# The first stage of a fused forward and backward kernel, put in another order

## The chip, the cores and the metric

The kernel runs on one core of a Trainium2 chip. A time is the device time of one execution in microseconds (us); the time of a kernel is the median over its runs. The core has five engines that take their instructions in a fixed order each: TensorE (PE, matrix products; PEld is its weight load), VectorE (DVE), ScalarE (ACT), GpSimd (POOL) and SyncE (SP), which here only issues DMA transfers. Instructions on different engines meet through semaphores.

## What is computed

The reference is a block with two branches, its output and the gradients with respect to every input. Cut to what matters:

```python
mod = (silu(c) @ w_mod).reshape(1, 6, 1, -1)
sa, ca, ga, sb, cb, gb = (mod[:, k] for k in range(6))
h = layernorm(x) * (1 + ca) + sa
x = x + ga * A(h)          # A: rfft2, times w_r + i w_i, irfft2
h = layernorm(x) * (1 + cb) + sb
x = x + gb * B(h)          # B: layernorm, w1 + b1, gelu, w2 + b2
out, vjp = jax.vjp(block, x, w_r, w_i, w1, b1, w2, b2, c, w_mod)
return out, *vjp(grad_out)
```

x and grad_out are 2048 x 1024, w_r and w_i 2048 x 513, w1 1024 x 3584, w2 3584 x 1024, w_mod 1024 x 6144, all bf16.

## The kernel before, in words

Everything is written for one core and runs as one stream of 6835 matmuls on PE with the other engines around it. A scheduler orders each engine's instructions by the program's text, by priorities (`tc.high_priority()` puts an instruction ahead) and by explicit edges: `tc.issue_after(ins)` puts what follows behind `ins` on its own engine. `nc.any` lets the scheduler choose between DVE and ACT. Tiles with the same tag share a buffer: a later one waits for the readers of the earlier one.

**The conditioning rows.** `mod_block(r, h)` (L247) multiplies the vector silu(c), spread over 128 partitions (`u_b`), with one 1 MB block of w_mod (`wblk`, a ring of three slots) into `pm`: eight matmuls (L253) and a copy (L256) to a row. r = 0 is sa, 1 is 1 + ca (`opca_row`), 2 ga, 3 sb, 4 1 + cb, 5 gb. All twelve blocks are loaded on SP's queue.

**The scaled copies of grad_out.** grad_out comes in four tiles `go` of 1 MB. PE turns each with 32 transposes of 128x128 into `pt` (L344). Each evicted tile is multiplied on the way by gb as a column (`gb_col`, from eight tiny matmuls `pc`, L337): even chunks by DVE (L347), odd ones by ACT (L351), 16 each. The result is `gBoT`, grad_out times gb, transposed.

**pp, the filler.** `ph_part(fc, js)` multiplies w2, transposed while it is loaded (`load_w2t`, L301, a DMA transpose on SP's queue into `wt`, two slots), with gBoT: eight matmuls (L684) for each of 28 chunks fc and four blocks j, 896 in all. An eviction (L691, L694) writes the tile to `pho`, and POOL's queue stores it to `d_ph` (L696). The first six chunks are the text ahead of the spectral stage, most of the others keep PE busy beside it.

**The row blocks of x.** `load_tok(i)` loads 512 rows of x: 256 directly by SP (L128), 256 gathered in reversed order by two indirect DMAs on POOL's queue (L131). For each block: mean and variance (`ln_dve` on DVE alone, L447; `ln_mix` half by DVE and half by ACT as sums and squares, L451 and L454), a square root on ACT (L427), the normalization on ACT (`norm_act`, L461, four per block), the product with 1 + ca on DVE, eight folds of 128x2048 on DVE (`fold_tok`, `fold_d`, all recorded at L173), and the addition of the folded sa (`saf`). The result is `fbuf[:, i]`.

**The matrices.** Sines and cosines of the transform are generated: POOL multiplies indices (L373), DVE takes them modulo a power of two (L396), ACT takes the sine (L397); eight 128x1024 passes into `smA`, `smB`, four 128x512 passes into `em1`, which POOL then scales (L412). They are stored to `d_SF` and `d_E`.

**The spectral stage** (`spectral_core`) begins with the products `pu` (L472) of the matrices with all four `fbuf` blocks, so it can begin only when the last block is folded. Then come pairs, `pv` and `po`; `consume_fwd(i)` takes each of four output blocks through two layer norms (on DVE and ACT, `ct` and `xt` tiles) and stores `d_x1` and `d_n3`.

**The MLP stage** follows a plan by hand, and PE's matmuls are strictly ordered there: z(0,0), the last 64 pp matmuls (fc 24 to 27, j = 2 and 3), z(0,1), z(0,2), z(0,3), b(0,0), z(0,4), b(0,1), z(0,5) and on. `z_block(b, g)` is 4 x 8 matmuls `pz` (L802) in two plus two PSUM banks; ACT evicts each with its bias (L805), squares (L807) and takes two sigmoids (L811, L813); DVE does the products of the gelu and its derivative, among them hh = sg * zb. Its five work tiles (`gt`) alternate between two sets. b(b, k) are parts of the product of hh with w2 (`pbo`, L853).

ACT holds one set of function tables at a time: sine, square root and sigmoid each need a table load (ACT_TABLE_LOAD) when another set is in.

Of the kernel before, what the change touches and what calls it, by code (L numbers as in the profile page):

```python
# [17 lines left out]
P = 128  # L18
# [17 lines left out]
def kernel(  # L36
# [88 lines left out]

    def load_tok(t4, src, i, eng=None):
        s3 = tok_flat(src)
        ins = (eng or nc.sync).dma_start(out=t4[:, 0:4:3, :],  # L128
                          in_=bass.AP(tensor=s3.tensor, offset=s3.offset + 128 * i * D, ap=[[D, P], [1024 * D, 2], [1, D]]))
        for q in range(2):  # L130
            nc.gpsimd.indirect_dma_start(out=t4[:, 1 + q, :], out_offset=None, in_=s3,  # L131
                                         in_offset=bass.IndirectOffsetOnAxis(ap=xidx[:, 2 * i + q:2 * i + q + 1], axis=0))
        return ins
# [113 lines left out]
    def mod_block(r, h, wblk=None):  # L247
# [4 lines left out]
        for jc in range(NDC):  # L252
            nc.tensor.matmul(pm[:], lhsT=u_b[:, jc, :], rhs=wblk[:, jc, :], start=(jc == 0), stop=(jc == NDC - 1))  # L253
        dst = MOD_DST[r][:, h * KH:(h + 1) * KH]
        with tc.high_priority():
            nc.any.tensor_copy(out=dst, in_=pm[:])  # L256
        if r in (1, 4):
            nc.vector.tensor_scalar(out=dst, in0=dst, scalar1=1.0, scalar2=None, op0=ALU.add)

# [40 lines left out]
    def load_w2t(fg):  # L300
# [4 lines left out]
    gos = [reg.tile([P, 4, D], BF16, name="go0", tag="px1")[:], reg.tile([P, 4, D], BF16, name="go1", tag="smb")[:],  # L305
           fbuf[:, 2], fbuf[:, 3]]
# [10 lines left out]
    mod_get(1, 0)  # L317
    load_tok(x4s[0], A_x, 0)
    mod_get(1, 1)
    mod_get(5, 0)  # L320
    for h in range(2):
        mod_block(1, h, wm[1, h][:])
    mod_get(5, 1)
    load_go(0)
    load_w2t(0)
    load_go(1)
    load_tok(x4s[1], A_x, 1)
    load_go(2)
    load_go(3)
    for h in range(2):  # L330
        mod_block(5, h, wm[5, h][:])
    load_tok(x4s[2], A_x, 2)
    load_tok(x4s[3], A_x, 3)
    load_w2t(1)
    pc = ps_d("pc")
    for cch in range(NDC):
        nc.tensor.matmul(pc[:, cch:cch + 1], lhsT=gb_row[0:1, cch * P:(cch + 1) * P], rhs=ones_bf[0:1, 0:1], start=True, stop=True)  # L337
    with tc.high_priority():
        nc.vector.tensor_copy(out=gb_col[:], in_=pc[:, 0:NDC])
    for j in range(4):  # L340
        for cch in range(NDC):
            pt = psum.tile([P, BW], BF16, tag="f", name="pt", bufs=4)
            for a in range(4):
                nc.tensor.transpose(pt[:, a * P:(a + 1) * P], gos[j][:, a, cch * P:(cch + 1) * P], ident[:])  # L344
            if cch % 2 == 0:
                with tc.high_priority():
                    nc.vector.tensor_scalar(out=gBoT[j][:, cch, :], in0=pt[:], scalar1=gb_col[:, cch:cch + 1], scalar2=0.0,  # L347
                                            op0=ALU.mult, op1=ALU.add, accum_out=gu[:, j, cch:cch + 1])
            else:
                with tc.high_priority():  # L350
                    nc.scalar.activation(out=gBoT[j][:, cch, :], in_=pt[:], func=ACT.Identity, scale=gb_col[:, cch:cch + 1],  # L351
                                         accum_out=gu[:, j, cch:cch + 1])

# [17 lines left out]
    def pts(out, in0, s1, s2, o0, o1=None):  # L371
        kw = {} if o1 is None else {"op1": o1}
        nc.gpsimd.tensor_scalar(out=out, in0=in0, scalar1=s1, scalar2=s2, op0=o0, **kw)  # L373
# [15 lines left out]
    def trig(dst, colv, rowv, nrow, width, modn, cosine):  # L389
# [3 lines left out]
        for r in range(nrow):  # L393
            pts(idx[:, r * width:(r + 1) * width], colv, rowv[:, r:r + 1], sh, ALU.mult, ALU.add)
        n = nrow * width
        nc.vector.tensor_scalar(out=idx[:, 0:n], in0=idx[:, 0:n], scalar1=modn - 1, scalar2=None, op0=ALU.bitwise_and)  # L396
        nc.scalar.activation(out=dst, in_=idx[:, 0:n].rearrange("p (r w) -> p r w", w=width), func=ACT.Sin,  # L397
                             bias=negpi[:], scale=2 * np.pi / modn)
# [5 lines left out]
    def gen_mats():  # L404
        for cl, colv, modn in ((CE, kevc, 2048), (SE, kev, 2048), (CO, kod, 4096), (SO, kod, 4096)):
            sm = (smA, smB)[cl % 2]
            for i2 in range(2):
                trig(sm[:, cl // 2, 2 * i2:2 * i2 + 2, :], colv, rown[:, 2 * i2:2 * i2 + 2], 2, 512, modn, cl < 2)
            nc.gpsimd.dma_start(out=d_SF[:, cl], in_=sm[:, cl // 2])
        for cl, colv, modn in ((CE, jf[:, 0:256], 1024), (SE, jf[:, 1:257], 1024), (CO, jod, 2048), (SO, jod, 2048)):  # L410
            trig(em1[:, 0, 2 * cl:2 * cl + 2, :], colv, rowd, 2, 256, modn, cl < 2)
        nc.gpsimd.tensor_scalar(out=em1[:, 1], in0=em1[:, 0], scalar1=2.0 / (S * D), scalar2=None, op0=ALU.mult)  # L412
        nc.gpsimd.tensor_scalar(out=em1[:, 1, 0:2, 0:1], in0=em1[:, 0, 0:2, 0:1], scalar1=1.0 / (S * D), scalar2=None, op0=ALU.mult)
        nc.gpsimd.tensor_scalar(out=em1[:, 1, 4:6, 255:256], in0=em1[:, 0, 4:6, 255:256], scalar1=1.0 / (S * D), scalar2=None, op0=ALU.mult)
        nc.gpsimd.dma_start(out=d_E[:], in_=em1[:])
# [42 lines left out]
    def norm_act(out4, in4, row, i):  # L458
        for q in range(4):
            t = 4 * i + q  # L460
            nc.scalar.activation(out=out4[:, q, :], in_=in4[:, q, :], func=ACT.Identity,  # L461
                                 scale=stats[:, row, 0, t:t + 1], bias=stats[:, row, 1, t:t + 1])
# [193 lines left out]
    for h in range(2):  # L656
        mod_block(0, h)
    gen_mats()
# [5 lines left out]
    nc.gpsimd.dma_start(out=out_7.rearrange("(c p) -> c p", p=P), in_=gb2r)  # L664
# [702 lines left out]
```

## Time and profile before

| | us |
|---|---|
| median of 3 runs (1461.4, 1461.49, 1465.73) | 1461.49 |
| the profiled execution | 1459.13 |
| its span in the trace | 1457.3 |
| its mean granted PE clock | 0.992 |

The profiled execution is 1.8 us longer than the span that the trace covers, and 2.4 us shorter than the median. Times inside the kernel are us from the start of the span.

The first stage, in the order of events:

| event | from | to |
|---|---|---|
| first pm matmuls, after 3.97 us of waiting for wblk | 6.32 | 9.89 |
| eight gathers of x issued on POOL | 4.74 | 14.57 |
| SP issues w2T for chunks 0 and 1 | 11.19 | 24.07 |
| transposes of grad_out on PE | 21.6 | 44.9 |
| first pp matmuls | 45.36 | |
| em scaled on POOL | 62.24 | 67.84 |
| norms of block 3 of x on ACT | 111.00 | 115.64 |
| last add into fbuf on DVE | 127.58 | 128.27 |
| first pu matmuls | 129.41 | |
| z(0,0) on PE | 343.87 | 350.77 |
| z(0,4) on PE | 389.19 | 396.10 |

A timeline row reads: start, duration, engine, line, operation, output<-input, shapes, how many instructions are put together in it, and in brackets how long the engine was idle before it and what released it.

### The profile page before, as it was taken

The numbers are of one execution on the slowest core, as the hardware profiler recorded it, in microseconds if no ns is written. First come the engines' busy times: TensorE is split into PE (matmuls) and PEld (weight loads), VectorE is DVE, ScalarE is ACT, GpSimd is POOL, SyncE is SP. The second block draws the span as 40 slices with busy tenths as digits, with TensorE's granted clock in tenths as the row PEclk, the third lists the DMA queues.
The fourth block names the chain that finished last, engine by engine and source line by source line (L and its number), as shares of the span: only waits on it lengthen the run. The fifth ranks groups of instructions, "written<-read, shape, count | busy, mean of one in ns | idle before, by whom it ended". The sixth has DMA issues, their size and how long they took to land. (4 is left out here: it accounts for less than half of the span.)

```text
span 1457.3 us, 18411 instructions
## 1 busy us (share of the span) xinstructions
PE 1396.5 (96%) x6835; PEld 649.0 (45%) x6835; DVE 1058.4 (73%) x1483; ACT 752.2 (52%) x1065; POOL 366.1 (25%) x441
## 2 busy tenths in 40 slices
PE   5889999999999999999999999999999999999997
PEld 2434545444444444444444444344444445444443
DVE  5884786898799787887520889898467678898650
ACT  4675555857887766665305574342622434344211
POOL 6520451211112122122211011021245441222432
PEclk8999999999999999999999999999999999999999
DMA  9962473899887877697998275297699987766991
GB/s 333 286 214 70 142 235 115 270 255 337 257 203 278 259 250 233 201 264 241 277 297 245 74 271 185 107 270 176 181 217 254 254 233 213 194 191 180 297 279 65
DMA packets 358367, 324.28 MB, mean 223 GB/s; under 512 B 209386, under 2 KB 301056, under 8 KB 358022
## 3 DMA queue, kind: packets, MB, share of 16 engines
q1 hardware_dynamic: 324166, 207.71, 52.7%
q0 software_dynamic: 34112, 115.41, 22.6%
q8 instruction: 53, 0.87, 0.2%
q14 instruction: 36, 0.29, 0.1%
HBM read 162.06 MB, written 111.20 MB: 188 GB/s over the span
## 5 line engine op out<-in xcount | busy, mean ns | idle before, releaser
L684 PE MATMUL pp<-gBoT,wt 128*128 128x512 bf16 x896 | 197.9, 380 | 4.5 <-DMA wt<-in_B_w_dram 2.6
L950 PE MATMUL pg<-w1T,gzr 128*128 128x512 bf16 x896 | 197.1, 381 | 0.2 <-ACT gn3b L961 0.2
L1266 PE MATMUL gw1acc<-gzh,n3n 128*128 128x512 bf16 x896 | 195.4, 379 | 1.3 <-DMA gzh<-d_gz 1.3
L684 PEld LDWEIGHTS <-wt 128*128 128x128 bf16 x896 | 87.7, 98 | 109.4 <-issue 4.2
L950 PEld LDWEIGHTS <-gzr 128*128 128x128 bf16 x896 | 87.3, 98 | 108.7 <-issue 6.6
L802 PEld LDWEIGHTS <-w 128*128 128x128 bf16 x896 | 87.3, 98 | 108.8 <-issue 4.7
L1266 PEld LDWEIGHTS <-n3n 128*128 128x128 bf16 x896 | 87.4, 98 | 106.1 <-issue 2.7
L802 PE MATMUL pz<-n3Tb,w 128*128 128x512 bf16 x448 | 99.2, 379 | 1.6 <-DVE w2sD L875 1.4
L802 PE MATMUL pz<-n3Ta,w 128*128 128x512 bf16 x448 | 98.7, 379 | 1.1 <-ACT gt L805 1.1
L1075 PE MATMUL gw2acc<-gB,hhsA 128*128 128x512 bf16 x448 | 98.5, 379 | 1.0 <-DMA hhsA<-d_hh 1.0
L853 PEld LDWEIGHTS <-hhA 128*128 128x128 bf16 x608 | 59.0, 98 | 71.7 <-issue 1.4
L805 ACT ACTIVATE gt<-pz,b_col 128x512 bf16<-128x512 f32 x112 | 72.5, 684 | 34.2 <-PE pz L802 32.8
L1270 ACT CAST gwo<-gw1acc 128x512 bf16<-128x512 f32 x50 | 29.1, 583 | 113.6 <-PE gw1acc L1266 99.0
L173 DVE TENSOR_TENSOR gt<-gt,gt 128x2048 bf16<-128x2048 bf16 x56 | 68.3, 1223 | 22.4 <-ACT gt L813 21.2
L1082 ACT CAST gwo<-gw2acc 128x512 bf16<-128x512 f32 x46 | 26.7, 583 | 109.9 <-PE gw2acc L1075 75.6
L811 ACT ACTIVATE gt<-gt 128x2048 bf16<-128x2048 bf16 x28 | 53.5, 1910 | 55.7 <-DVE gt L173 55.7
L173 DVE TENSOR_TENSOR ct<-ct 128x2048 bf16<-128x2048 bf16 x64 | 75.9, 1218 | 1.8 <-DMA d_n<-ct 1.1
L1075 PEld LDWEIGHTS <-hhsA 128*128 128x128 bf16 x448 | 43.6, 98 | 53.0 <-DMA hhsA<-d_hh 1.7
L997 DVE CUSTOM_DVE_ANT_0 otl<-otl 128x1024 bf16<-128x1024 bf16 x24 | 29.1, 1223 | 49.9 <-DMA otl<-in_w_mod_dram 44.2
L807 ACT ACTIVATE gt<-gt 128x2048 bf16<-128x2048 bf16 x28 | 53.4, 1908 | 5.4 <-DVE hhC L173 2.5
L813 ACT ACTIVATE gt<-gt 128x2048 bf16<-128x2048 bf16 x28 | 53.5, 1909 | 0.5
L1271 POOL DMA_DIRECT2D out_dram<-gwo x56 | 30.6, 548 | 85.6 <-ACT gwo L1270 53.4
(325 smaller groups left out, 2531.5 us busy)
## 6 DMA issues: line engine op xcount, KB each, us to landing
gzr<-d_gz SPq DMA_DIRECT2D x28, 512.0 KB
wblk<-in_w_mod_dram SPq DMA_DIRECT2D x12, 1024.0 KB
out_dram<-otl POOLq DMA_DIRECT2D x48, 256.0 KB
out_dram<-gwo POOLq DMA_DIRECT2D x96, 128.0 KB
d_ph<-pho POOLq DMA_DIRECT2D x21, 512.0 KB
d_hh<-hhA POOLq DMA_DIRECT2D x19, 512.0 KB
w2sD<-in_B_w_dram SPq DMA_DIRECT2D x14, 512.0 KB
hhC<-d_ph SPq DMA_DIRECT2D x14, 512.0 KB
```

Of the source, the lines that this page charges most:

```text
L173: return nc.vector.tensor_tensor(out=out, in0=a, in1=b, op=op)
L684: last_pe[0] = nc.tensor.matmul(pp[:], lhsT=wt[:, fg % 2, cch, k * P:(k + 1) * P], rhs=gBoT[j][:, cch, :], start=(cch == 0), stop=(cch == ...
L802: last_pe[0] = nc.tensor.matmul(pz[:], lhsT=w1s[g][:, cch, k * P:(k + 1) * P], rhs=n3T[:, cch, :], start=(cch == 0), stop=(cch == NDC - 1))
L805: nc.scalar.activation(out=zb[:, k, :], in_=pz[:], func=ACT.Identity, bias=b1_col[:, fc:fc + 1], scale=1.0)
L807: nc.scalar.activation(out=av, in_=zb, func=ACT.Square)
L811: nc.scalar.activation(out=sg, in_=bv, func=ACT.Sigmoid, scale=2.0 * GK)
L813: nc.scalar.activation(out=bv, in_=bv, func=ACT.Sigmoid, scale=-2.0 * GK)
L853: last_pe[0] = nc.tensor.matmul(pbs[i][:], lhsT=hh[:, k, i * P:(i + 1) * P], rhs=wp[:, k, :], start=False, stop=(g == 6 and k == 3))
L950: last_pg[0] = nc.tensor.matmul(pgs[i][:], lhsT=gzs[b, g][:, k, i * P:(i + 1) * P], rhs=w1Ts[g][:, k, h * KH:(h + 1) * KH], start=(g == 0 ...
L1075: nc.tensor.matmul(acc[:], lhsT=hh_of(fc)[:, t, :], rhs=gBs[t // 4][:, t % 4, h * KH:(h + 1) * KH], start=(t == 0), stop=(t == NT - 1))
L1266: nc.tensor.matmul(acc[:], lhsT=n3ns[t // 4][:, t % 4, cch * P:(cch + 1) * P], rhs=gz2[t // 8][:, t % 8, :], start=(t == 0), stop=(t == NT ...
L1271: nc.gpsimd.dma_start(out=out_4[cch * P:(cch + 1) * P, fg * 512:(fg + 1) * 512], in_=ob)
```

## The change

- SP's order: both blocks of gb's row first, then x's block 0, the four tiles of grad_out, the two blocks of 1 + ca, w2T 0, x's blocks 1 to 3, w2T 1, and then the blocks of sa.
- POOL makes the index passes of four of the sine matrices first, and then issues the eight gathers of x.
- ACT takes four sines, then makes its 16 scaled copies, and only then block 0's norm. The copies of gb's second block and of 1 + ca are DVE's.
- pp for chunks 0 and 1 alternate (j by j), right behind the two blocks of 1 + ca on PE. All pp evictions of the first eight chunks are ACT's; `nc.any` remains for the others.
- The blocks of sa follow chunk 1; the six late conditioning blocks come in twos after chunks 3, 4 and 5, where they came in threes after chunks 3 and 5. ACT copies these.
- The matrices are generated in parts: four passes at the start, four after block 1's norm, the four of em1 after block 2's. The four stores to d_SF stand behind them in the text. ACT scales em1, where POOL did.
- Block 1 of x has its statistics from DVE alone. Explicit edges put block i's statistics and norm behind block i - 1's folds and norm.
- saf is added to the blocks 0 and 1 together after block 1.
- The zeroing of `css` goes from POOL to DVE, behind the last fold; the store of out_7 goes behind that of d_E; the slots of the grad_out tiles change.

```diff
-    mod_get(1, 0)
-    load_tok(x4s[0], A_x, 0)
-    mod_get(1, 1)
     mod_get(5, 0)
-    for h in range(2):
-        mod_block(1, h, wm[1, h][:])
     mod_get(5, 1)
-    load_go(0)
-    load_w2t(0)
-    load_go(1)
-    load_tok(x4s[1], A_x, 1)
-    load_go(2)
-    load_go(3)
...
+    rows_of = gen_rows()
+    for _ in range(4):
+        next(rows_of)
+    with tc.issue_after(gen_in["pool"].ins):
+        load_tok(x4s[0], A_x, 0)
+    for j in range(4):
+        load_go(j)
+    for h in range(2):
+        mod_get(1, h)
+    load_w2t(0)
+    mod_block(5, 0, wm[5, 0][:])
+    with tc.issue_after(gen_in["dve"].ins):
+        mod_block(5, 1, wm[5, 1][:], nc.vector.tensor_copy)
...
+            if j % 2 == 0:
+                with tc.high_priority():
+                    (nc.scalar.copy if fc < 8 else nc.any.tensor_copy)(out=ov, in_=pv)
...
+            else:
+                with tc.high_priority(), tc.issue_after(act_in.ins):
+                    act = nc.scalar.activation(out=gBoT[j][:, cch, :], in_=pt[:], func=ACT.Identity, scale=gb_col[:, cch:cch + 1],
+                                               accum_out=gu[:, j, cch:cch + 1])
...
+    for j in range(4):
+        act_in, go_dve = go_turned(j)
+    with tc.issue_after(act_in.ins), tc.issue_after(gbc_in.ins):
+        ln_dve(x4s[0], 0, 0)
+        act_go = norm_act(fbuf[:, 0], x4s[0], 0, 0)
+    with tc.issue_after(gen_in["pool"].ins):
+        for i in range(1, 4):
+            load_tok(x4s[i], A_x, i)
+    x_gathers = g_in[0]
+    with ordered():
+        for h in range(2):
+            last_pe[0] = mod_block(1, h, wm[1, h][:], nc.vector.tensor_copy)
+    for j in range(4):
+        for fc in range(2):
+            ph_part(fc, (j,))
+    load_w2t(1)
...
     for fc in range(PH_EARLY):
-        ph_part(fc, (0, 1, 2, 3))
+        if fc > 1:
+            ph_part(fc, (0, 1, 2, 3))
+        if fc == 1:
+            with ordered():
+                for h in range(2):
+                    last_pe[0] = mod_block(0, h, wm[0, h][:], nc.scalar.copy)
...
         if fc % 2 == 1:
             load_w2t(fc // 2 + 2)
-            if fc > 1:
-                with tc.issue_after(last_pe[0].ins):
-                    for r, h in late_mods[3 * (fc // 2 - 1):3 * (fc // 2)]:
-                        mod_block(r, h)
-
+        if fc > 2:
+            with ordered():
+                for r, h in late_mods[2 * fc - 6:2 * fc - 4]:
+                    last_pe[0] = mod_block(r, h, None, nc.scalar.copy)
...
     for i in range(4):
         x4, fb = x4s[i], fbuf[:, i]
-        if i == 0:
-            with tc.issue_after(u_in.ins):
-                ln_dve(x4, 0, i)
-        elif i > 0:
-            ln_mix(x4, 0, i, fb)
-        else:
-            ln_act(x4, 0, i, fb)
-        norm_act(fb, x4, 0, i)
+        if i > 0:
+            with tc.issue_after(act_go.ins), tc.issue_after(folds[i - 1].ins):
+                (ln_mix(x4, 0, i, fb) if i > 1 else ln_dve(x4, 0, i))
+                act_go = norm_act(fb, x4, 0, i)
+        if i == 1:
+            with tc.issue_after(act_go.ins), tc.issue_after(x_gathers.ins):
+                for _ in rows_of:
+                    pass
+        elif i == 2:
+            with tc.issue_after(act_go.ins), tc.issue_after(x_gathers.ins):
+                gen_cols()
+                d_E_in = gen_store()
```

160 lines of the change are left out of this document (82 added, 78 removed).

## The prediction

> **What bounds the kernel now.** I read the profile in this order: busy time by engine, the 40 slices, a table of stretches, the waits of TensorE (PE), and then single stretches of the timeline.
>
> ```profile
> PE 1396.5 (96%) x6835; PEld 649.0 (45%) x6835; DVE 1058.4 (73%) x1483; ACT 752.2 (52%) x1065; POOL 366.1 (25%) x441
> PE   5889999999999999999999999999999999999997
> DMA  9962473899887877697998275297699987766991
> ```
>
> PE is busy 96%; its only poor slices are the first three (110 us). So the end moves with PE's matmul stream, and a gain lasts only if PE never waits for it again later.
>
> ```profile
> 0.00:20.00 20.00, 8.95 (x22) 2.95 (x23) 10.61 (x28) 3.23 (x5) 16.58 (x35) 0.95 0.93 327
> 20.00:46.00 26.00, 15.99 (x152) 11.15 (x151) 18.43 (x52) 21.47 (x43) 8.80 (x12) 0.84 1.11 300
> 46.00:92.00 46.00, 38.28 (x170) 16.52 (x169) 37.51 (x58) 34.32 (x48) 25.65 (x26) 0.97 0.91 288
> 92.00:129.40 37.40, 36.80 (x168) 16.38 (x167) 33.20 (x37) 18.44 (x29) 2.13 (x4) 0.99 0.35 113
> ```
>
> Columns: stretch, length, busy PE, PEld, DVE, ACT, POOL with counts, clock, DMA share, GB/s. Before 20 us PE has data for only 9 us; to 46 us DMA is full (1.11). From 92 us PE is full.
>
> ```profile
> 45.36 4.91 PE L684 MATMUL pp<-gBoT,wt 128*128 128x512 bf16 x22 [0.43 <-DVE gBoT L347]
> ...
> 127.58 0.69 DVE L173 TENSOR_TENSOR fbuf<-fbuf,sb_saf 128x1024 bf16<-128x1024 bf16 x1
> ```
>
> pp, the stream that fills PE, starts at 45.36, held by the scaled copies. The last add that the spectral matmuls pu (L472) need ends at 128.27; they start at 129.41, PE having waited 0.60 of that.
>
> **Prices.** Warm 512-wide matmuls run at 0.216 us (64 in 350.77 to 364.59); a cold group of 8 takes 3.57 instead of 1.73. ScalarE rows: norm 1.23, sine 1.14 or 0.71, pp eviction 0.58, copy of gB^T 0.68 + 0.20, table load 1.28, sum or square 1.06 to 1.15 + 0.19. DVE: 4096-wide 2.29, 2048-wide 1.2.
>
> **The change, part by part.**
>
> 1. *gb and grad_out first.* SP now issues: gb's two blocks, x0, the four grad_out blocks, w_mod(1) twice, then w2T 0. That is 11 MB with the eight gathers; the traces' 12 to 24 us stretch moves 0.37 to 0.40 MB per us, so all but w2T is in at about 31 to 34 us. gb's row is ready at about 15 (its second copy stands behind the fourth index pass on DVE: eight POOL passes of 0.91 each, which are now ahead of the gathers, whose first issue moves from 4.74 to some 13.5). Transposes and copies end near 29, limited by grad_out's arrival and by 16 copies x 0.88 = 14.1 us on ScalarE, 16 on DVE; before, the end was 45. Taken: 29; bounds 27 to 34.
>
> 2. *pp starts.* It needs w2T 0. Before, SP spent 12.88 us (from 11.19) issuing that DMA transpose and nothing waited for it at 45; when it lands the trace does not show. Bounds: 33, when the bytes ahead are in and it comes free, and 45. I take 38.5: the bytes, then 3.5 to 6 us (40 to 46 us in the trace, with w2T 1 alone, moved only 134 to 147 GB/s). Gain in start: 45.36 - 38.5 = 6.9, less 2.3 for a cold restart.
>
> 3. *More pp ahead of pu.* By the instruction orders of both kernels, 321 pp matmuls stand ahead of pu, 264 before: 57 x 0.216 = 12.3 us more PE work done in the first stage, and as much less between the last po and z(0,0). PE's floor to pu: 38.5 + (321 + 64) x 0.216 + 2.3 = 124.
>
> 4. *ScalarE carries the stage.* It alone evicts pp for fc < 8. Between pp's start and pu its order holds 16 norms (19.7), eight sums and squares (10.3), 8 sines (7.4), 5 table loads (6.4), about 40 evictions (23.2), 8 mod copies (4.6), the scaling of em (about 2): 74 us in 90. Each is in a fixed order, and x0's norm stands behind the first pp eviction (about 42, a PE that starts at 38.5); so x0 is done at 48, x1 at 58 (its norm waits for x0's folds on DVE, which are 13 us: 2.29 + 8 x 1.2 + 0.7), x2's squares wait about 3 us for the folds of x1 and its norm ends near 92, em's scaling at 104, x3's norm at 115. Then 2.29 + 8 x 1.18 + 0.69 and gaps, as in the trace (115.67 to 128.27): fbuf 3 at 128, pu at 129. Before: 129.41. DVE gains 3.5 us (a fold beside POOL's 5.60 us scaling took 4.67, others 1.2), but it is not what ScalarE waits for at that place. So the 12.3 us of part 3 are gained, and pu is not earlier. Bounds for pu: 124 (PE's floor) and 134 (w2T at 45 less what slack is left).
>
>    Table loads ahead of pu: 7 for 4, 3 x 1.28 = 3.8 us by rows. The Trainium skill, "ScalarE: Activation LUTs", section "What ACT_TABLE_LOAD costs", counts 1283 ns and a drain of 1380 ns for each switch, by estimate about 8 us for three; the trace has the load at 1.28, and the next activation 0.01 to 0.02 us behind it, so it does not show the drain. By the page pu would be some 4 us later; I go by the row.
>
> 5. *Where the 12.3 us arrive.* pu to the last po has the same filler in both orders, so the token blocks leave it at the same time: x1's block 3 is ready on DVE at 341.2 (before's clock). z(0,0) starts at Z = 343.87 - 12.3 - 0.4 = 331. That brings z's matmuls forward, not the block chain, and ScalarE has to evict both.
>
> ```profile
> 379.97 1.91 ACT L811 ACTIVATE gt<-gt 128x2048 bf16<-128x2048 bf16 x1 [1.01 <-DVE gt L173]
> 381.79 0.67 ACT L805 ACTIVATE gt<-pz,b_col 128x512 bf16<-128x512 f32 x1
> 382.36 1.23 ACT L461 ACTIVATE ct<-ct,stats 128x1024 bf16<-128x1024 bf16 x1
> 383.49 1.25 ACT L805 ACTIVATE gt<-pz,b_col 128x512 bf16<-128x512 f32 x2
> ...
> 388.03 1.25 ACT L461 ACTIVATE ct<-ct,stats 128x1024 bf16<-128x1024 bf16 x1
> 389.16 1.91 ACT L813 ACTIVATE gt<-gt 128x2048 bf16<-128x2048 bf16 x1
> ```
> ```profile
> 385.73 3.63 PE L853 MATMUL pbo<-w2sA,hhB 128*128 128x512 bf16 x16
> 389.19 7.07 PE L802 MATMUL pz<-n3Ta,w 128*128 128x512 bf16 x32
> 400.84 1.46 PE L802 MATMUL pz<-n3Ta,w 128*128 128x512 bf16 x6 [1.12 <-ACT gt L805]
> ```
>
>    These rows show it: z(0,3)'s evictions (L805 at 383.5) are threaded between block 3's last norms (L461), so z(0,4) starts at 389.19 with a free PSUM bank and without a wait. In the changed order they stand behind all four of these norms, behind a sqrt that waits for block 3's statistics, behind a table load and behind two sigmoids. In time from Z: block 3's first sum stands behind the fifth pp eviction after z(0,0): 7.1 + 5 x 1.73 = 15.8; its norms (threaded with z(0,1) and z(0,2), 34.5) end at 40.6; two 2.28 us products, eight statistics and z's products take 13.2 (before: 363.3 to 376.2 = 12.9), so the sqrt is at 53.8; square 1.9 and four norms 5.0 with gaps: 61.6; table and sigmoid 3.2: 64.8; sigmoid 1.9: 66.7; first z(0,3) eviction: 67.4. PE wants that bank at Z + 47. z(0,4) starts at 331 + 67.4 = 398.4 for 389.19: **+9.2**, after 20 us without work.
>
> 6. *Behind it.* Cold restart: 3.57 - 1.73 = +1.8. Three waits of PE that follow in the trace (1.12 at 400.84, 0.16, 1.39 at 467.47) vanish, since ScalarE is then ahead of PE: -2.7. The orders are the same from there on.
>
> Edits at nothing: late mods in twos (the same 48 matmuls in a full PE; w_mod's ring of three slots now gets three, then two, then three loads; cover: pp, of which PE has 40 tiles; without it one wblk wait of up to 3.97 as at 6.32), css on DVE (after the last fold, needed only by the first pair), out_7 later (nothing reads it), gos in other slots.
>
> Sum: +9.2 + 1.8 - 2.7 = +8.3. On the profiled execution's 1459.13 that is 1467.4; the median is 1461.49, 2.4 above it, so on the median's footing 1469.8. I state **1469**.
>
> **Rivals.**
>
> *A. PE sets the time all through (the other side).* If ScalarE reaches z(0,3)'s evictions by Z + 47, the first stage's 12.3 us stay. The point that decides is the gap between Z + 47 and the first L805 of z(0,3). For: PE is 96% busy and before's order has no such wait; ScalarE is only 52% busy. Against: its order is fixed, and block 3's chain ended at 389 before with Z at 343.87, which leaves no slack for a Z 12 us earlier. Price: -12.3 to -17 (pu at PE's floor): 1461.5 - 12.5 = 1449.
>
> *B. The gain is given back evenly (it doesn't do what it says).* If block 3's chain from pu on is 5 us shorter, through a pu at 124 and a DVE with 13 evictions less (13 x 0.68), z(0,4) starts at about 389 to 393: -1 to +3. For: the offsets from 15.8 to 67.4 add rows of two engines, and some of these may overlap. Against: in before the same chain ran without slack to 389. Price: 1460 to 1464.
>
> *C. pu later.* w2T 0 at 45, SP and DMA full as at 20 to 46 us (share 1.11), d_SF stores in the same time: pu at 134, everything behind it 5 later: 1474.
>
> *D. Wider stall.* Two more waits of PE for ScalarE in the first stage, each like the 1.45 at 76.64 (the trace's only one of PE for ScalarE's evictions there): +2.9, 1472. It lies within the likeliest case's own range.
>
> **Chances.** Likeliest case (with D) 0.46, C 0.12, B 0.17, A 0.25. About 0.3% (4.4 us) is what a measurement of this kernel can tell from no change: its three runs lie 4.3 apart. The likeliest case's own range is 1463 to 1476. B straddles the lower border of slower, C is slower: slower 0.58, same 0.17, faster 0.25. The 8-in-10 range takes in C (1474 + 5) and most of A: 1447 to 1479.
>
> **What would show it.** Part 1: the last gB^T copy before 32 us; pc near 15. Part 2: first pp at 36 to 41, waiting for DMA wt. Part 4: first pu at 127 to 131, waiting for DVE fbuf, and PE waits for ScalarE's pho or phr around 105 to 114. Part 5: the first z(0,0) matmul near 331; one PE wait of 15 to 22 us for ACT gt at z's evictions (line 850 after), ending near 398. Wrong if that wait is under 8 us (A or B), or if pu starts before 125 or after 133.

## The result and the profile after

The changed kernel takes 1485.87 us (median of five runs, 1483.12 to 1487.45) where the kernel before takes 1461.49 (five runs, 1459.19 to 1465.73): a ratio of 1.0152, 95% interval 1.0125 to 1.0179, which is 18.3 to 26.2 us. It is slower; the two medians lie 24.4 us apart. Here and below the ratios leave out slow executions (one of l_before, one of l_after), which the medians include. The prediction said slower, 1469, and a range to 1479; the time lies 6.9 above that range. The profiled execution took 1486.42, its span 1484.6, 27.3 longer than the span before.

The first three fences are of the changed kernel: busy time and slices from the page, a table of stretches (columns as in the prediction), and PE's timeline.

```profile
PE 1395.5 (94%) x6705; PEld 649.9 (44%) x6835; DVE 1053.7 (71%) x1475; ACT 759.7 (51%) x1076; POOL 361.4 (24%) x437
...
PE   5989989998499999999999999999999999899997
...
DMA  9963473989567687597999265396699988676994
```

```profile
0.00:20.00 20.00, 10.81 (x73) 6.35 (x74) 12.18 (x29) 11.10 (x17) 17.23 (x36) 0.93 0.92 333
20.00:46.00 26.00, 17.92 (x126) 9.92 (x126) 19.59 (x57) 14.11 (x30) 7.17 (x10) 0.92 1.09 315
46.00:92.00 46.00, 45.51 (x208) 20.36 (x212) 35.95 (x54) 34.28 (x51) 14.70 (x15) 1.00 0.89 283
92.00:129.40 37.40, 31.54 (x136) 13.78 (x137) 26.36 (x28) 26.80 (x42) 11.31 (x14) 0.91 0.45 141
...
386.00:420.00 34.00, 15.33 (x67) 6.44 (x68) 25.27 (x35) 22.78 (x21) 2.30 (x3) 0.75 0.43 148
```

PE's busy time stands at 1395.5 us, where it was 1396.5, but 130 of its 6835 matmuls have no record in this trace; two kernels below with the same order on PE and with every record show 1400.2 (e_w1all) and 1406.4 (e_dnpool). So most of the 27.3 us, though not all, is idle time of PE. The slices say where: digit 2 is better than before (9 for 8), and a new hole, the digit 4, stands at 371 to 408 us. In the stretches PE has 11.0 us more busy time up to 92 us (74.24 against 63.22), loses 5.3 of it again up to 129.4, and from 386 to 420 is busy for 15.33 us out of 34, at a clock of 0.75.

```profile
39.63 10.53 PE L474 MATMUL pp<-gBoT,wt 128*128 128x512 bf16 x47 [1.91 <-DMA wt<-in_B_w_dram]
...
101.76 1.01 PE L533 MATMUL pu<-smA,fbuf 128*128 128x512 bf16 x2 [5.76 <-DVE fbuf L175]
...
109.06 23.47 PE L474 MATMUL pp<-gBoT,wt 128*128 128x512 bf16 x105
...
133.45 6.86 PE L533 MATMUL pu<-smA,fbuf 128*128 128x512 bf16 x31
...
333.44 7.07 PE L847 MATMUL pz<-n3Ta,w 128*128 128x512 bf16 x32
...
352.19 8.58 PE L474 MATMUL pp<-gBoT,wt 128*128 128x512 bf16 x31 [4.77 <-ACT pho L481]
...
379.80 8.43 PE L847 MATMUL pz<-n3Ta,w 128*128 128x512 bf16 x31 [4.34 <-ACT gt L850]
...
410.68 8.35 PE L847 MATMUL pz<-n3Ta,w 128*128 128x512 bf16 x31 [18.57 <-ACT gt L850]
```

Read against before's events: pp starts 5.7 us earlier, pu 4.0 later, z(0,0) 10.4 earlier, z(0,4) 21.5 later. In between lie the waits of PE for ScalarE, the last of them 18.57 us. ScalarE's timeline ahead of it, from block 2's square root (L404) and block 3's first sum (L428) on:

```profile
340.34 0.30 ACT L404 ACTIVATE mv<-mv,eps_c 128x4 f32<-128x4 f32 x1 [7.68 <-DVE mv L432]
...
358.00 1.06 ACT L428 ACTIVATE ct<-xt 128x1024 bf16<-128x1024 bf16 x1 [1.80 <-DVE xt L175]
...
387.35 1.28 ACT L404 ACT_TABLE_LOAD   x1
396.77 0.30 ACT L404 ACTIVATE mv<-mv,eps_c 128x4 f32<-128x4 f32 x1 [8.14 <-DVE mv L415]
...
400.41 4.62 ACT L438 ACTIVATE ct<-ct,stats 128x1024 bf16<-128x1024 bf16 x4
405.05 1.28 ACT L856 ACT_TABLE_LOAD   x1
406.35 3.71 ACT L856 ACTIVATE gt<-gt 128x2048 bf16<-128x2048 bf16 x2
409.96 2.40 ACT L850 ACTIVATE gt<-pz,b_col 128x512 bf16<-128x512 f32 x4
```

This is the order that the prediction described: square root, four norms, table load, two sigmoids, and only then z(0,3)'s evictions (L850). But ScalarE itself had waited for VectorE: 7.68 us for block 2's statistics (mv), 1.80 for block 3's x1 ahead of the first sum, and 8.14 for its statistics ahead of the square root. So the question is why block 3 is late on VectorE. Its timeline, first before, then after; `xt<-ct,xt` is the addition that completes x1 of a block, here of blocks 2 and 3, and the row between begins block 3's unfolding (the first two rows after, the memset of css and the last addition into fbuf, are taken up below):

```profile
315.06 2.29 DVE L173 TENSOR_TENSOR xt<-ct,xt 128x4096 bf16<-128x4096 bf16 x1
...
321.10 1.23 DVE L173 TENSOR_TENSOR ct<-ct 128x2048 bf16<-128x2048 bf16 x1 [0.50 <-DMA d_n<-ct]
...
338.99 2.28 DVE L173 TENSOR_TENSOR xt<-ct,xt 128x4096 bf16<-128x4096 bf16 x1
```
```profile
128.93 1.77 DVE L769 MEMSET cs<- 128x2056 uint32 x1 [0.38 <-issue]
130.61 0.63 DVE L175 TENSOR_TENSOR fbuf<-fbuf,sb_saf 128x1024 bf16<-128x1024 bf16 x1
...
324.72 2.29 DVE L175 TENSOR_TENSOR xt<-ct,xt 128x4096 bf16<-128x4096 bf16 x1
...
338.40 1.23 DVE L175 TENSOR_TENSOR ct<-ct 128x2048 bf16<-128x2048 bf16 x1 [7.14 <-DMA d_n<-ct]
...
355.68 2.29 DVE L175 TENSOR_TENSOR xt<-ct,xt 128x4096 bf16<-128x4096 bf16 x1
```

Block 2 is 9.7 us later than before, block 3 is 16.7 later. The 7.0 between them are nearly all in one bracket: the unfolding overwrites a `ct` buffer out of which block 1's n3 is still being stored, and waits 7.14 us for that store to land (before: 0.50). SP's queue shows the store (d_n<-ct) among its neighbours, before and after:

```profile
314.42 0.39 SPq L740 DMA_DIRECT2D d_n<-ct  x1
314.91 16.45 SPq L301 DMA_TRANSPOSE wt<-in_B_w_dram  x2
331.46 15.43 SPq L757 DMA_DIRECT2D w<-in_B_w_dram  x5
```
```profile
309.12 12.57 SPq L304 DMA_TRANSPOSE wt<-in_B_w_dram  x2
321.86 0.46 SPq L802 DMA_DIRECT2D w<-in_B_w_dram  x1
325.15 0.38 SPq L785 DMA_DIRECT2D d_n<-ct  x1
325.59 16.48 SPq L802 DMA_DIRECT2D w<-in_B_w_dram  x4
```

Before, the store is issued first and the two w2T transposes and the w1 loads follow. After, the buffers of w2T and w1 come free earlier, so two transposes and a 1 MB load of w1 are issued ahead of the store. The store itself also comes 10.7 us later, when ScalarE has finished block 1's norm. Issue to the row that waits: 6.7 us before (314.42 to 321.10), 13.2 after (325.15 to 338.40). While VectorE stood there, what followed in its order stood too: block 2's last statistics (L432) came at 340.14, and ScalarE had waited 7.68 us for them.

### The profile page after: what moved, and what is told of

Read it like the earlier page. It is cut to its first block, busy times and chain, and to the rows that moved or that the text cites. A ratio compares the mean times of both kernels' runs of the same rounds, so it can differ in the third digit from the quotient of the medians.

```text
span 1484.6 us, 18273 instructions
## 1 busy us (share of the span) xinstructions
PE 1395.5 (94%) x6705; PEld 649.9 (44%) x6835; DVE 1053.7 (71%) x1475; ACT 759.7 (51%) x1076; POOL 361.4 (24%) x437
## 3 DMA queue, kind: packets, MB, share of 16 engines
q1 hardware_dynamic: 324166, 207.71, 51.6%
## 5 line engine op out<-in xcount | busy, mean ns | idle before, releaser
L850 ACT ACTIVATE gt<-pz,b_col 128x512 bf16<-128x512 f32 x112 | 72.5, 683 | 34.5 <-PE pz L847 32.9
L1315 ACT CAST gwo<-gw1acc 128x512 bf16<-128x512 f32 x50 | 28.9, 583 | 116.6 <-PE gw1acc L1311 99.5
```

Of the source, the lines that this page charges most:

```text
L850: nc.scalar.activation(out=zb[:, k, :], in_=pz[:], func=ACT.Identity, bias=b1_col[:, fc:fc + 1], scale=1.0)
```

## The experiments

Fifteen kernels were run. "x1" is the start of block 3's addition on VectorE, "mark" the start of the second group of `pa` matmuls (L917; L872 before), late in the MLP stage of the first block: behind it the orders on PE, VectorE and ScalarE are before's in every kernel. Both are read in the profiled execution of each kernel. The kernels from e_tail on were measured in groups of four, four, four and three, in the table's order, each with the kernel before beside them: its medians were 1463.16, 1467.3, 1465.22 and 1466.63.

| kernel | median | ratio, 95% | x1 | z(0,4) | mark |
|---|---|---|---|---|---|
| before | 1461.49 | | 339.0 | 389.2 | 521.5 |
| after | 1485.87 | 1.0152 (1.0125 to 1.0179) | 355.7 | 410.7 | 541.9 |
| e_tail | 1486.12 | 1.0153 (1.0118 to 1.0188) | 355.9 | 397.9 | 543.4 |
| e_bsig | 1469.59 | 1.0036 (1.0015 to 1.0058) | 337.3 | 389.2 | 519.8 |
| e_pp264 | 1479.67 | 1.0096 (1.0067 to 1.0126) | 350.5 | 399.1 | 532.6 |
| e_css | 1477.25 | 1.0076 (1.0043 to 1.0109) | 341.2 | 389.0 | 525.1 |
| c_before | 1466.28 | 1.0006 (0.9979 to 1.0032) | 338.1 | 387.9 | 520.4 |
| c_shift | 1468.52 | 1.0020 (0.9999 to 1.0040) | 338.0 | 390.6 | 522.2 |
| e_w1hold | 1487.36 | 1.0152 (1.0120 to 1.0184) | 356.0 | 411.0 | 542.3 |
| e_cols3 | 1478.93 | 1.0072 (1.0040 to 1.0105) | 350.1 | 396.3 | 532.3 |
| e_dnpool | 1487.82 | 1.0138 (1.0089 to 1.0186) | 351.5 | 406.5 | 538.2 |
| e_w1all | 1486.08 | 1.0134 (1.0085 to 1.0182) | 350.0 | 405.2 | 536.4 |
| e_cssact24 | 1486.23 | 1.0126 (1.0080 to 1.0171) | 360.2 | 406.3 | 541.0 |
| b_act24 | 1478.26 | 1.0089 (1.0056 to 1.0122) | 347.5 | 391.3 | 527.5 |
| l_before | 1469.35 | 0.9997 (0.9964 to 1.0030) | 336.8 | 397.5 | 526.7 |
| l_after | 1472.36 | 1.0036 (1.0011 to 1.0062) | 357.5 | 400.2 | 535.0 |
| l_css | 1461.32 | 0.9964 (0.9942 to 0.9986) | 341.4 | 389.9 | 519.6 |

The expectations number the theories as they arose. Theory 1 is the prediction's part 5: the order on ScalarE is the price. 5a is the w1 load ahead of block 1's store, 6 the share of pp's evictions on VectorE.

**Is it ScalarE's order?** e_tail is the changed kernel with block 3's second norm and store put behind the sigmoids of z(0,1); the tile `hhA`, which shares a buffer with block 3's data, is allocated behind them too. e_bsig puts the opposite into the kernel before: a sigmoid of z(0,1) behind block 3's last norms.

```diff
# e_tail (on after)
-        ln_dve(tmp, 2, i)
-        norm_act(tmp, tmp, 2, i)
-        nc.sync.dma_start(out=chunk_rows(d_n3, i), in_=tmp)
+        def second_norm(): ...
+        if i < 3:
+            second_norm()
+        else:
+            tail[0] = second_norm
...
+            if (b, g) == (0, 2):
+                with tc.issue_after(sig_in[1].ins):
+                    tail[0]()
# e_bsig (on before)
-            with after_ev():
+            with tc.issue_after(n3_in[0].ins) if n == 1 else after_ev():
                 nc.scalar.activation(out=sg, in_=bv, func=ACT.Sigmoid, scale=2.0 * GK)
```

> The changed kernel with one move: the sqrt, norm and store of block 3 (last layer norm) stand on ScalarE behind the two sigmoids of z(0,1), everything before that in the same order. Theory 1 (ScalarE's order holds PE): z(0,3)'s evictions come at about 391 instead of 410, PE's wait of 18.6 us before z(0,4) falls under 4 us; the moved 8 us of ScalarE work are met again later in part, so 10 to 18 us come back: ratio to before 1.003 to 1.008 (changed kernel 1.0152). Rival (block 3's lateness itself, through its DMA stores, holds PE): the wait only moves to z(0,5) or the next block, ratio 1.012 or more.

> The kernel before with one edge: ScalarE takes z(0,1)'s sigmoid only behind block 3's last norms, as the changed kernel does. First stage untouched. Theory 1: z(0,3)'s first eviction moves from 383.5 to about 390, z(0,4) from 389.2 to about 391.5 to 394 with a PE wait for ScalarE of 2 to 5 us that was not there: ratio 1.0015 to 1.0035. Rival (that order costs nothing where block 3 is early enough): no new wait of PE, ratio 0.999 to 1.001.

PE's timeline of e_tail:

```profile
397.94 9.94 PE L854 MATMUL pz<-n3Ta,w 128*128 128x512 bf16 x32 [5.38 <-ACT gt L857]
...
432.15 8.18 PE L854 MATMUL pz<-n3Ta,w 128*128 128x512 bf16 x24 [10.45 <-ACT gt L857]
```

z(0,4) starts 12.7 us earlier, and a second wait of 10.45 us follows; together the two waits are 15.8 us for 18.57, the mark is no earlier (543.4), and the time is the same as after's. The stall moved, as the rival said. e_bsig brings a wait of 1.94 us and no later mark (519.8); that its ratio came out at the edge of theory 1's range is therefore luck. So ScalarE's order sets where PE stops, not how much it loses: theory 1 falls as the cause. (e_bsig's median is nonetheless 6.4 above before's; its mark says that this lies behind 520 us, see below.)

**Is it PE running ahead?** e_pp264 holds pp from chunk 8 on behind pu, so that the extra pp work of the first stage is given up.

```diff
+        with tc.issue_after(first_pu[0].ins) if fc == PH_EARLY + 2 else ExitStack():
-        ph_part(fc, (0, 1, 2, 3) if fc < PH_KEEP else (0, 1))
+            ph_part(fc, (0, 1, 2, 3) if fc < PH_KEEP else (0, 1))
```

> The changed kernel with chunks 8 and later of pp held behind the first full group of pu, so that 264 pp matmuls stand ahead of pu as in before, and z(0,0) comes late again. PE loses the 12.3 us that the first stage had gained. Theory 1 (a z(0,0) that runs ahead of block 3's chain gains nothing and brings the bad order and the collisions): pu at about 131, z(0,0) near 347, no wait over 4 us before z(0,4), ratio 1.001 to 1.006, so faster than the changed kernel although PE does less ahead of pu. Rival (the first stage's 12.3 us are a gain that something else outweighs): they are lost on top, ratio 1.022 to 1.025.

```profile
351.23 7.07 PE L851 MATMUL pz<-n3Ta,w 128*128 128x512 bf16 x32
...
399.11 7.07 PE L851 MATMUL pz<-n3Ta,w 128*128 128x512 bf16 x32
```

In its PE timeline z(0,0) starts 17.8 us later than in the changed kernel and z(0,4) 11.6 earlier, without a wait in its row. PE idles 12.14 us ahead of pu, and the kernel still takes less than the changed one: a ratio of 1.0096 for 1.0152, and a mark 9.3 us earlier. Neither expected range was met. The work brought forward did not pay. But this edit changed the orders of VectorE and ScalarE as well, so the run does not put a price on the 12.3 us alone.

**Is it one small edit?** e_css puts the zeroing of css back on POOL. e_cols3 does that too, and makes em1 after block 3's norm.

```diff
# both
-    with tc.issue_after(folds[4].ins):
-        nc.vector.memset(css[:], 0.0)
+    nc.gpsimd.memset(css[:], 0.0)
# e_cols3 alone
-        elif i == 2:
+        elif i == 3:
             with tc.issue_after(act_go.ins), tc.issue_after(x_gathers.ins):
                 gen_cols()
```

> The changed kernel with css zeroed by GpSimd again, as in before: DVE's 1.77 us memset no longer stands ahead of the last add into fbuf. Also, in the order that results, z(0,3)'s evictions stand ahead of block 3's last two norms. Theory 1: pu 2 us earlier (131), PE's wait before z(0,4) 8 us or less, ratio 0.995 to 1.005. Rival (the memset is worth its 2 us and no more, since block 3 is late for other reasons): ratio 1.013 to 1.014.

> The changed kernel with css zeroed by GpSimd (as in an earlier run, pu at 130.4 and 1.0076) and the four passes of em1 with em's scaling, their two table loads and the d_E store moved behind block 3's norm. Theory 3 (ScalarE's order paces the first stage): about 10 us of ScalarE work go from between block 2's and block 3's norms, fbuf 3 is ready 6 to 10 us earlier, pu at 121 to 125, everything to z(0,4) earlier by as much: ratio 0.998 to 1.003. Rival (VectorE's folds or PE's pp stream set pu): pu at 128 or later, ratio 1.006 to 1.009.

e_css, PE's timeline:

```profile
130.37 9.88 PE L533 MATMUL pu<-smA,fbuf 128*128 128x512 bf16 x45
...
389.03 8.75 PE L846 MATMUL pz<-n3Ta,w 128*128 128x512 bf16 x32 [3.36 <-ACT gt L849]
```

VectorE's timeline of e_css, the unfolding of block 3 and its x1:

```profile
325.82 1.22 DVE L175 TENSOR_TENSOR ct<-ct 128x2048 bf16<-128x2048 bf16 x1 [1.14 <-DMA d_n<-ct]
...
341.15 2.29 DVE L175 TENSOR_TENSOR xt<-ct,xt 128x4096 bf16<-128x4096 bf16 x1
```

The first long run of po on PE, in the kernels before, after and e_css:

```profile
230.71 8.46 PE L630 MATMUL po<-gm,V 128*128 128x256 bf16 x76
```
```profile
236.84 8.46 PE L691 MATMUL po<-gm,V 128*128 128x256 bf16 x76
```
```profile
233.44 8.46 PE L691 MATMUL po<-gm,V 128*128 128x256 bf16 x76
```

From there to block 3's x1 it is 108.3 us before, 118.8 after and 107.7 in e_css. One memset moved from one engine to another takes back 16.8 of the 20.4 us at the mark (in the median 10.3 of 24.4, and neither expected ratio was met). Its own 2.2 us (1.77 and 0.38 idle) can't do that. The scheduler, given this one difference, orders PE otherwise far behind it: 302 pp matmuls ahead of pu, not 321, and from 200 us on the same alternation of po and pp as in the kernel before. e_cols3, with the same memset on POOL, gets a third order and a mark at 532.3, though its pu starts at 129.2. On PE it is close to that of e_css, but VectorE has 13 of the po evictions in place of 9, and the stretch to x1 takes 115.3 us; so PE's order alone is not what counts. Its rival's ranges were met (pu at 128 or later, 1.006 to 1.009). The start of pu decides little; the orders in the consume stage decide much.

**Is it the start time alone?** c_before is the kernel before once more, c_shift the same with one pp tile computed twice (eight matmuls, 1.73 us).

```diff
-            for cch in range(NDC):
+            for cch in list(range(NDC)) * (2 if (fc, j) == (23, 1) else 1):
```

> The kernel before, unchanged, as a control with a profile of its own: all theories say ratio 1.000. From its second profile: how much the stretch from the second pa group (521.5 us) to the end, 935.8 us before and 941 to 951 in five other profiles with the same order of instructions there, varies without any change.

> The kernel before with one pp tile ahead of z(0,0) computed twice: 8 more matmuls, 1.73 us, and nothing else. If the stretch from 520 us to the end depends on how its transfers happen to meet (theory 4: any change of phase there costs 5 to 10 us, since DMA is at 0.9 and more of its time and the orders are fixed), ratio 1.004 to 1.008. Rival (the stretch is steady, and the 5 to 15 us in the other kernels have a cause of their own): ratio 1.0005 to 1.002.

z(0,0) starts where it does in c_before (342.6), z(0,4) is 2.7 us later and the mark 1.8; the median is 1.2 above its group's. The ratio lies in the rival's range, not in theory 4's: this small delay was passed on as it is and tipped nothing over, though the order of some VectorE and ScalarE instructions changed with it.

**Is it the queue ahead of the store?** e_w1hold holds w1 groups 1 to 6 until block 3's unfolding, e_dnpool stores block 1's n3 through POOL's queue, e_w1all puts all w1 loads behind that store on SP.

```diff
# e_w1hold
-        with tc.issue_after(w2t_in[0].ins):
+        with tc.issue_after(w2t_in[0].ins if g == 0 else unf_in[0].ins):
# e_dnpool
-        nc.sync.dma_start(out=chunk_rows(d_n3, i), in_=tmp)
+        (nc.gpsimd if i == 1 else nc.sync).dma_start(out=chunk_rows(d_n3, i), in_=tmp)
# e_w1all
-        with tc.issue_after(w2t_in[0].ins):
+        with tc.issue_after(w2t_in[0].ins), tc.issue_after(dn_in[1].ins):
```

> The changed kernel with the same order on PE, ScalarE and VectorE; only the loads of w1's groups 1 to 6 on SP wait until VectorE has begun block 3's first unfold, that is until block 1's store to d_n3 has landed. Theory 2 (the store landed late, 13.2 us after its issue for 6.7 before, because five 1 MB loads of w1 that a PE further ahead had released were in flight with it): VectorE's wait of 7.1 us for that store falls to about 1 us, block 3's x1 is ready at about 349 instead of 357.9, and PE's waits at z(0,0) to z(0,4) (28 us) shrink by 6 to 9: ratio 1.009 to 1.012 (changed kernel 1.0152). Rival (what delays the store is ahead of it on the queue, the two transposed loads of w2): the wait stays at 5 us or more and the ratio at 1.014 to 1.016.

> The changed kernel with block 1's store to d_n3 issued on GpSimd's queue in place of SP's. Theory 5 (that store, which VectorE's unfold of block 3 waits for 7.1 us, lands late because it stands behind two transposed loads of w2 and a load of w1 on the same queue): it lands within 8 us of its issue, VectorE's wait falls under 3 us, block 3's x1 is ready 4 to 7 us earlier (351 to 354), and the end is earlier by the same 4 to 7: ratio 1.011 to 1.013. Rival (all queues share what the transposed loads leave): wait 5 us or more, ratio 1.014 to 1.016.

> The changed kernel with all loads of w1, the first of them included, behind block 1's store to d_n3 on SP's queue; the two transposed loads of w2 stay ahead of it. Theory 5a (the one 1 MB load of w1 ahead of the store is what delays it): VectorE's wait falls from 7.1 to 2 to 4 us, block 3's x1 3 to 5 us earlier. Theory 5b (the transposed loads ahead of it are): the wait stays at 6 to 7 us. Ratio 1.012 to 1.014 by 5a, 1.015 by 5b.

VectorE's timeline of e_w1all:

```profile
331.02 1.23 DVE L175 TENSOR_TENSOR ct<-ct 128x2048 bf16<-128x2048 bf16 x1 [2.74 <-DMA d_n<-ct]
...
350.03 2.28 DVE L175 TENSOR_TENSOR xt<-ct,xt 128x4096 bf16<-128x4096 bf16 x1
```

The loads issued behind the store are not the cause (e_w1hold: the wait is 6.38 for 7.14, the mark unchanged). The one load of w1 issued ahead of it is a part of it: behind the store, the wait falls to 2.74, x1 comes 5.7 us earlier and the mark 5.5. Another queue helps less (e_dnpool: 5.74 of wait, x1 4.2 and the mark 3.7 earlier).

Both profiles were ahead before their edit could act: the long run of po starts at 234.80 in e_w1all and 234.63 in e_dnpool, 2.0 and 2.2 us ahead of after's 236.84, in the same order on PE. From there to x1 it is 118.8 us after, 118.1 in e_w1hold, 116.9 in e_dnpool and 115.2 in e_w1all, where before has 108.3. So the load of w1 answers for some 3.6 of the 10.6 us and the queue for 2.0; that e_dnpool's x1 fell into its range is luck. In e_w1all PE in turn waited 4.30 us for the load of w1 at z(0,0), and its wait at z(0,4) was 19.92. In these two the medians did not fall in step: 20.9 and 22.6 above their group's before, where after has 24.4; the intervals overlap.

**Is it VectorE's load?** Evictions of pp are split by the scheduler. e_cssact24 gives all those below chunk 24 to ScalarE, with the memset on POOL; b_act24 does the like in the kernel before. The three l kernels leave out the product with 1 + cb and the addition of sb in `consume_fwd` (eight VectorE instructions of 2.28 us), so h of the second branch is not scaled or shifted: l_before, l_after, and l_css, which also has the memset on POOL.

```diff
# e_cssact24; b_act24 has 8 <= fc < 24 for nc.any
-                    (nc.scalar.copy if fc < 8 else nc.any.tensor_copy)(out=ov, in_=pv)
+                    (nc.scalar.copy if fc < 24 else nc.any.tensor_copy)(out=ov, in_=pv)
# l_before, l_after, l_css
-        tt(tmp, tmp, bcn(opcb_row, 4), ALU.mult)
-        tt(tmp, tmp, bcn(sb_row, 4), ALU.add)
```

> The changed kernel with css zeroed by GpSimd and with ScalarE evicting all pp tiles of chunks 0 to 23, where the scheduler gave some 15 of those beside the x1 chain to VectorE. Theory 6 (VectorE is the bound of the chain from po to block 3's x1: 101 to 107 us busy of 110 to 121, of it 10 to 12 us pp evictions): that stretch falls from 110.0 to about 100 us, z(0,0) is limited by PE again, waits before z(0,4) and z(0,5) (3.36 and 3.28 us with css alone) go, ratio 0.996 to 1.003 for 1.0076. Rival (ScalarE, with 10 us more, becomes the bound): ratio 1.007 or more.

> The kernel before with ScalarE evicting the pp tiles of chunks 8 to 23. Theory 6: VectorE's chain to block 3's x1 is about 10 us shorter here too, but z(0,0) is set by PE in this kernel and waits for nobody, so only the few waits behind it (1.1 to 1.5 us) can go: ratio 0.997 to 1.001. Rival (the chain, not PE, sets the z stage in before as well): z(0,4) 5 us or more earlier, ratio 0.993 to 0.996.

> The kernel before without the product with 1 + cb and the addition of sb in the x1 chain (8 VectorE instructions of 2.28 us, 18 us in all; the second branch's input and what follows from it change). Theory 7 (the end stands at block 3's x1 plus 182 us, unless PE's own work sets it): block 3's x1 comes about 12 us earlier, but z(0,0) stays at 342 to 344, where PE's work puts it; its waits behind z(0,3) go: second pa group at 518 to 520, ratio to before 0.997 to 1.000. Rival (the chain alone sets the z stage): 510 or earlier.

> The changed kernel without the same 8 instructions. Theory 7: its z(0,0) is 9 to 10 us earlier than before's (333 to 334) by the first stage's gain, and the lighter chain now lets PE use a part of it: second pa group at 512 to 522 where the changed kernel had 541.9, so 20 to 30 us earlier for 18 us of VectorE work left out, ratio to before 0.995 to 1.003, equal to or faster than the lighter kernel before. Rival (the first stage's gain is lost for a reason outside this chain): pa at 528 or later, ratio 1.006 or more.

> The changed kernel without these 8 instructions and with css zeroed by GpSimd, so that the order from pu to z(0,0) is before's. Theory 7: z(0,0) at about 339 by PE's work, no wait over 2 us behind it, second pa group at 515 to 518, 2 to 4 us ahead of the lighter kernel before: ratio 0.995 to 0.999. Rival as for the one before.

Moving evictions off VectorE makes both kernels' x1 later (360.2, 347.5), so theory 6's forecast fails. The rival, that ScalarE becomes the bound, fits: in both, VectorE waits 6.3 us for ScalarE's square root (before and e_css 0.8). The two runs don't show what VectorE's evictions alone are worth. Leaving VectorE's work out does little for block 3 either: by x1, three blocks have been through, six instructions or 13.7 us less, and x1 is 2.2 us earlier in l_before and 1.8 later in l_after. l_after's timelines of VectorE and PE:

```profile
334.96 1.23 DVE L175 TENSOR_TENSOR ct<-ct 128x2048 bf16<-128x2048 bf16 x1 [17.86 <-DMA d_n<-ct]
```
```profile
337.44 17.04 PE L474 MATMUL pp<-gBoT,wt 128*128 128x512 bf16 x70 [11.16 <-DVE pho L484]
```

Here block 2's x1 is done early (314.81, after: 324.72), and VectorE then stands 17.86 us at the store; the pp evictions queued behind it on VectorE hold PE for 11.16. The work saved became waiting. l_before has a wait of 8.79 of the same kind, and z(0,0) comes at 352.21 there, after PE has waited 8.7 us for VectorE in pp. Theory 7 missed all three marks (518 to 520, 512 to 522, 515 to 518); l_before's ratio lies in its range with a mark 5.2 us later than before's, which is luck. l_css, where the store wait is 4.6 and PE has no wait of over 1.0 us behind z(0,0), is the fastest kernel here, though not a version of the whole computation: against its group 0.9964, where l_before has 0.9997. The intervals overlap, and l_before's PE was held up where that of l_css was not, so the pair does not show what the first stage is worth. No run here shows a gain from the changed first stage alone.

**What holds over most runs.** The mark minus x1 is 182.1 to 184.2 in before, c_before, c_shift, e_bsig, e_css, e_pp264 and e_cols3, and 186.2 to 187.6 in after, e_tail, e_w1hold, e_w1all and e_dnpool, which share after's order on PE. In these twelve, whatever PE had done in the first stage, the MLP stage begins in earnest when block 3 is through VectorE. The other five lie apart: 180.7 in e_cssact24, 180.0 in b_act24, 178.2 in l_css and 177.6 in l_after, and 189.9 in l_before, where x1 is early and PE comes late to z(0,0). So x1 is not the only gate.

## Why the prediction was right in part, and where it failed

| step | predicted | measured |
|---|---|---|
| 1: pc; last copy to gB^T | 15; 29 | 15.05; 29.97 |
| 2: first pp, waiting for wt | 38.5 | 39.63, waiting for wt |
| 3: pp ahead of pu | 321 | 321 |
| 4: pu | 129 | 133.45 |
| 5: z(0,0) | 331 | 333.44 |
| 5: x1 of block 3 ready | 341.2 | 357.97 |
| 5: block 3's first sum on ScalarE | 346.8 | 358.00, waiting for x1 |
| 5: one long wait, z(0,4) | 15 to 22, at 398.4 | 18.57, at 410.68 |
| 6: mark or sum | +8.3 | +20.4 at the mark, +24.4 in the median |

**Parts 1 to 3** held within 1.2 us. (The rate of 0.37 to 0.40 MB per us that part 1 goes by holds from 12 to 22 us in the kernel before; from 22 to 24 us it was 0.34.)

**Part 4** took the order of ScalarE rightly: block 3's norm starts at 111.05, as in the kernel before (111.00); it ends at 116.6, where the text had 115. It then lost 4 us in two places. "css on DVE (after the last fold, needed only by the first pair)" stood among the edits at nothing; the memset stands ahead of block 3's last addition, which ends at 131.24 (128.27 before). And PE itself was not there sooner: it had waited 5.76 us at 101.76 for block 2's folds, then ran 105 pp matmuls without a gap until 132.4, so PE was the last to come, 1.1 us behind the addition. The wait expected there, for ScalarE's evictions at 105 to 114, did not occur. Rival C has the right size (134), by another cause: w2T landed at 39.6, not at 45.

**Part 5** is where the prediction failed, in one sentence: "pu to the last po has the same filler in both orders, so the token blocks leave it at the same time". They leave it 16.7 us later: 4.0 from pu, 2.1 from pu to the long run of po (101.3 us before, 103.4 after), and 10.6 from there to x1. Of the 10.6, 7.3 are waits for n3 stores (8.4 us against 1.1 in VectorE's table of waits for 285 to 365) and 3.4 are VectorE work, since more of the evictions fell to it (pp 12.3 for 10.1 us, po 7.3 for 6.1). These are the sizes of the rows, not shown prices: e_w1all had 5.1 us less of store waits and got 3.6 back. e_css, with another order, got back all of the 10.6. The same filler does not mean the same order, and the text had followed PE, ScalarE and VectorE, but not SP's queue with the stores in it.

The wait at z(0,4) then came as described, in its place and by its releaser, but on a later block 3: 21.5 us instead of 9.2. The prediction let block 3's chain start behind ScalarE's fifth pp eviction, at 346.8. In the run that eviction ended at 356.2, since ScalarE had stood 7.68 us for VectorE's statistics of block 2, and the first sum waited 1.80 more for x1, until 358.00. From that first sum to z(0,3)'s first eviction the prediction had 51.6 us, and the run took 52.0: the chain was sized rightly, its start was wrong. That the wait's length fell into its range is luck: PE, forecast to stand from Z + 47 on, had lost 9.8 us to three shorter waits for ScalarE by then and came to z(0,4) at 392.1 in place of 378. Against the kernel before, x1 is 16.7 of the 21.5 and the stretch from x1 to z(0,4) 4.8 (50.2 before, 55.0 after). That 4.8 goes with the changed order; e_tail shows that it can't be had back by re-ordering ScalarE alone.

**Part 6** was near: restart 1.3 (8.35 for 7.07 us, with one matmul's record missing) for 1.8, two of the three waits behind it gone and the third down from 1.39 to 0.63; from z(0,4) to the mark the lateness changes by -1.1 for the -0.9 predicted.

**The rivals.** A, that PE sets the time all through, named the gap between z(0,0) + 47 and z(0,3)'s first eviction as the point that decides: it is 333.4 + 47 = 380.4 against 409.96, so A is wrong. B needed a shorter block chain, and it is longer. D's waits for ScalarE came in the z stage (4.77, 0.72, 4.34), not in the first stage.

**What stays open.** Which detail makes the scheduler choose the other order was not found; e_css shows that the memset suffices, not why. And the stretch behind the mark, with the same order on PE, VectorE and ScalarE, takes 935.8 us in before's profile, 942.0 in c_before's, 942.7 in after's, 950.8 in e_bsig's and 957.3 in e_dnpool's. The profiles put some of this to waits for transfers (hhsA, gzh, otl, w2sC). Of the 27.3 us between the two profiles 6.9 lie there, and c_before, the same kernel as before, has 6.2 of them too, so they need no cause in the change; the 20.4 at the mark lie within the measured 18.3 to 26.2. Not explained are e_bsig and e_css: their medians stay 6.4 and 14.1 above before with marks 1.7 earlier and 3.6 later.

## What to carry to other kernels

Work brought forward on the busiest engine counts only if the chain that gates the next stage comes forward too; here PE gained 10 us at z(0,0) and lost 21 at z(0,4). When loads are released earlier, follow each queue that they share with stores, down to the instruction that overwrites a stored buffer, and to what is queued behind that instruction. With a scheduler that orders all engines, one moved memset can re-order a stage up to 200 us later, so compare the orders and not the diff.

## What the runs showed of the hardware

- The same 1 MB store of n3 landed, from its issue to the start of the instruction that waits for it, in 6.7 us (before), 7.7 (e_css, 318.16 to 325.82), 7.8 (e_w1all, 323.19 to 331.02), 13.2 (after) and 18.7 (l_after, 316.21 to 334.96). In after a load and two DMA transposes were issued ahead of it; in l_after another transpose (of block 0's n3) and a load of x were ahead and the two transposes right behind it, and it was slower still. In before, too, the two transposes were right behind it. Position in the queue alone does not explain this. Nor did another queue free the store: through POOL's it took 11.6 us (e_dnpool, 323.22 to 334.80), and VectorE still waited 5.74 us for it. That agrees with the Trainium skill, "DMA: Bandwidth & Descriptors", section "Issuing engines are not separate DMA queues", by which transfers run on the same 16 DMA engines and interleave, whichever engine starts them.
- A table load took 1.28 us and the next activation began 0.01 to 0.02 us behind it (405.05 + 1.28 = 406.33, next at 406.35). The Trainium skill, "ScalarE: Activation LUTs", section "What ACT_TABLE_LOAD costs", adds a drain of 1380 ns to each switch; by the estimate worked out from it pu would be some 4 us later, and pu was 4.4 later than predicted. The trace does not agree on the cause: no such gap is seen behind its loads or ahead of them (0.02 us), and block 3's norm, behind the last of them, began on time (111.05).
- PE came back cold: 8.35 us for 31 matmuls recorded behind the wait of 18.57 us, where 32 warm ones take 7.07. The granted clock was 0.84 over these 8.2 us and 1.00 over the next group (422.31 to 429.22).
